# Weight conversion without its shared buffer, transposes of k and q in one buffer, and another order of a pair's steps, in a fused attention and channel-mixing kernel on one core

## The chip, the cores and the metric

The kernel runs on one core of a Trainium2 chip. Its time is the device time of the core in microseconds, and the time of a kernel is the median over its runs. Before the change three runs took 1230.66, 1232.53 and 1235.76 us. The lowest lies 0.15% below the median.

## The reference

Eight batches of eight heads, 576 tokens, head width 64. Each head goes through an attention with exponential features, the heads are laid side by side to 512 channels, and two mixing steps follow, one over tokens (rank 32) and one over channels (512 to 2048 to 512).

```python
def phi(x):
    proj = np.einsum('bhsd,df->bhsf', x, w_phi)              # 128 features
    proj = proj - np.max(np.abs(proj), axis=-1, keepdims=True)
    return np.concatenate([np.exp(proj), np.exp(-proj)], axis=-1)
q_p, k_p = (phi(q), phi(k))
kv = np.einsum('bhsf,bhsd->bhfd', k_p, v)
z = np.sum(k_p, axis=2)
num = np.einsum('bhsf,bhfd->bhsd', q_p, kv)
den = np.einsum('bhsf,bhf->bhs', q_p, z)[..., None] + 1e-06
x = num / den                                   # then heads to channels
h = x.transpose(0, 2, 1) @ U @ V                # over tokens
u = x + h.transpose(0, 2, 1)
out = u + np.maximum(u @ w_ch1, 0.0) @ w_ch2    # over channels
```

q, k, v and w_phi come as 32-bit floats. U, V, w_ch1 and w_ch2 come as 64-bit floats, which the chip converts itself from their words.

## The kernel before

**Pairs.** A `Pair` is two heads of one batch; there are 32, four to a batch. Its steps are: load of raw k and q (L250, L257); `transpose_k` (a small transpose tT of the 64 last tokens, and T0, k with features on partitions) and `transpose_q` (T1, the same of q); `s_k0` and `s_k1` (projection matmuls pkt and pk, then maxima, differences and exponentials of k); `s_kv` (kv_ps, the sums over tokens); `s_q0` and `s_q1` (pq, and the features of q, with the maximum over partitions on POOL, L342, and its subtraction on DVE, L343); and `s_out` (matmuls xp, then the division into x). From batch 2 on (`split`) a float is carried as two rounded parts: T is copied to a rounded upper half by ACT (L275), and the rest is written by DVE (L276). T0 and T1 have a buffer each (tags T0 and T1, L311).

**Tokens.** For a batch whose four pairs are done, `split` writes x as two parts (xs, three buffers of the group "wide" at a time), `down` multiplies with U (pp, kept as pst, L551 and L552), `up` multiplies with V (vp) and adds to x (L565), which also goes to memory.

**Mixer.** u is transposed (pt, split into uT_hi and uT_lo), then 16 pieces of 128 hidden channels follow. `hidden(f)` is a chunk of 12 matmuls into ph, from which ACT makes h_hi (L599) and DVE h_lo (L600). `add(f)` is a chunk of 12 matmuls into the four banks o. A batch thus has 32 chunks, kept in a list `todo`, from which `mix(n)` takes the next n. There are nine mixers: one a batch, and one for the last 64 tokens of all batches (x_tail).

**Weights.** `weight_blocks` converts 32 blocks of 128 by 512 words (m = 1, 2 and f = 0 to 15). A block is loaded from SP into a buffer of "wide" (512 KB, L216 or L220). ACT (L141, L145) and DVE (L142, L147, L150) take the words apart, POOL adds the two pieces (L155, INT64_ADD), ACT rounds the upper part w_hi (L226) and DVE writes the rest w_lo (L227). The piece that L147, L150 and L155 work on is w_r, one buffer for all blocks, so L147 of a block comes after L227 of the block before. "wide" has three buffers, which also hold xs and, at the end of each batch, the saved u (st).

**What sets the order.** Batches 0 and 1, with the weights, are ordered on every engine by a scheduler that simulates the program. From pair 8 on (`ordered`), the order on TensorE is the one written out: between two steps of the pairs stand one or two chunks of the batch before, and at a batch's end (`boundary`) the last three chunks alternate with the transposes of the next mixer. The other engines are still ordered by the scheduler. An engine runs its instructions strictly in its order. "cur", "nxt" and "far" are the pair that gives its output, the next, and the one after.

PSUM has eight banks: three of the group "at" (everything of the pairs and of Tokens, in turn), one ph, four o.

Of the kernel before, what the change touches and what calls it, by code (L numbers as in the profile page):

```python
# [20 lines left out]
P = 128  # L21
# [4 lines left out]
def tile_kernel(  # L26
# [96 lines left out]
    NW = 3  # L123
# [85 lines left out]
    def weight_blocks():  # L209

        for f in range(NFC):
            fs = slice(f * P, (f + 1) * P)
            for m in (1, 2):
                st = wide(f"w{m}_{f}", (C, 2), I32)
                if m == 1:
                    nc.sync.dma_start(  # L216
                        out=st.rearrange("p (c n) w -> p c n w", c=NCC),
                        in_=w1[:, fs].rearrange("(c p) n w -> p c n w", c=NCC))
# [7 lines left out]
                nc.scalar.copy(out=hi, in_=r)  # L226
                nc.vector.tensor_sub(lo, r, f32(hi))  # L227
                w_hi_t[m, f], w_lo_t[m, f] = hi, lo
            yield f
# [9 lines left out]
    class Pair:  # L239
# [38 lines left out]
        def transposes(self):  # L278
            self.transpose_k()
            self.transpose_q()  # L280

        def transpose_k(self):

            nm = self.nm
            tT = self.ps("tT", True)
            nc.tensor.transpose(out=tT[:, 0:2 * ST], in_=self.t_r, identity=ident)
            dt = F32R if self.split else F32
            self.tail_T = att.tile([P, 2, P], dt, tag="tail_T", name=f"tail_T{nm}")
            if not self.split:
                nc.gpsimd.memset(self.tail_T, 0.0)  # L290
            self.T = [self.transpose(0)]
# [11 lines left out]
        def transpose(self, n):  # L303
# [6 lines left out]
            if self.split:  # L310
                m = att.tile([P, 2, SM], F32R, tag=f"T{n}", name=f"T{n}_{self.nm}")  # L311
                for s in range(2):
                    self.stack(pT[s * D:(s + 1) * D, :], m[:, s, :])
            else:
                m = att.tile([P, SM], F32, tag=f"T{n}", name=f"T{n}_{self.nm}")
                nc.scalar.copy(out=m, in_=pT)
# [252 lines left out]
    class Mixer:  # L569
# [35 lines left out]
        def add(self, f):  # L605
            if self.o is None:
                self.o = [ps(f"o{self.g}_{t}", "o") for t in range(4)]
            terms = self.h.pop(f)
            for t in range(4):
# [11 lines left out]
            if f == NFC - 1:  # L621
                self.finish()

        def finish(self):
            g = self.g
            for t in range(4):
# [7 lines left out]
                if t % 2 == 1:  # L634

                    tails = out[2 * t - 2:2 * t + 2, SM:S, :].rearrange(
                        "(t s) r e -> s r t e", s=2)
                    for s in range(2):
                        nc.sync.dma_start(
                            out=tails[s], in_=self.x[s * ST:(s + 1) * ST, t - 1:t + 1, :])  # L640
# [20 lines left out]
    def mix(n=1):  # L661
        for _ in range(n):
            if todo:
                fn, f = todo.pop(0)
                if fn.__self__.g == 0 and done_f[0] < NFC:
                    weights(f + 2)
                fn(f)
# [81 lines left out]
    def boundary(m, up=None, far=None):  # L749

        mix(len(todo) - 3)
        m.transposes(0)
        m.transposes(1)
        mix()
        m.transposes(2)
        mix()
        if up is not None:
            up(NT)
        m.transposes(3)
        mix()  # L760
        todo.extend(m.chunks())
        mix()
        if far is not None:
            far.transpose_q()

    def ordered(cur, nxt, x, xt, tk):

        for n, (b, j) in list(enumerate(pairs))[ORDERED * NPAIR:]:
# [10 lines left out]
            mix()  # L779
            do(nxt, "s_k1")  # L780
            mix()
# [8 lines left out]
            if j == 1:  # L790
                tk.down(0)
            if last:
                mix()
                tk.down(1)
            do(nxt, "s_q1")
            do(far, "transpose_k")
            mix()
            if last:
# [13 lines left out]
            else:  # L812
                do(far, "transpose_q")
                mix(2 if j == 2 else 1)
# [6 lines left out]
    if True:  # L821
# [4 lines left out]
        cur.transposes()  # L826
# [4 lines left out]
        nxt.transposes()  # L831
# [6 lines left out]
        for n, (b, j) in enumerate(pairs[:ORDERED * NPAIR]):  # L838
# [5 lines left out]
            if nxt.split:  # L844
                step(nxt.s_k1)
            step(narrow, nxt, cur, x, xt)
            if j == 1:
                tk.split(0)
            if j == NPAIR - 1:
                fill = [nxt.s_q0] + ([nxt.s_q1] if nxt.split else []) + [far.transposes]  # L850
# [7 lines left out]
            else:  # L858
# [3 lines left out]
                step(far.transposes)  # L862
            cur, nxt = nxt, far
        with tc.manual_schedule(engines={nc.tensor.engine}):
            mix(3)
# [32 lines left out]
```

## Time and profile before

| what | us |
|---|---|
| runs: lowest, median, highest | 1230.66, 1232.53, 1235.76 |
| the profiled execution, as a run | 1234.6 |
| its span in the trace | 1232.8 |
| TensorE busy (PE) | 1159.0 |
| VectorE busy (DVE) | 652.4 |
| ScalarE busy (ACT) | 534.7 |
| GpSimd busy (POOL) | 197.0 |
| mean granted clock of TensorE | 0.982 |

The span is what the trace covers; 1.8 us of the run lie around it. TensorE is busy almost throughout, yet not evenly: the page's row of 40 slices is well under full in the first quarter and full after it. In the first 280 us lie batches 0 and 1, the loading and conversion of the weights and all 32 chunks of the first mixer; the rest is batches 2 to 7 in the hand-written order (to about 1005 us) and, behind them, the last mixers alone. A row of a timeline gives the start in us, the duration in us, the engine, the line, the operation and tiles, and in brackets how long the engine stood idle before it and what ended that.

### The profile page before, as it was taken

Reading aid. Unit: us, or ns where it says so; the run is one execution under the profiler, and the core shown is the slowest. Engines: PE = TensorE matmul, PEld = TensorE weight load, DVE = VectorE, ACT = ScalarE, POOL = GpSimd, SP = SyncE. Lnnn points to the kernel's source line nnn. Section 1 sums busy time; section 2 is a strip of 40 time slices with the busy share of each in tenths; the row PEclk is TensorE's granted clock in tenths of the full one; section 3 lists DMA queues with packets and bytes.
Section 4 is the critical chain, followed back from the end, with each engine's and each line's share of the span. In section 5 each row is a group of like instructions: output and inputs, shape, how many; then the busy total and the mean of one; then the engine's idle time right before and its main releaser. Section 6 shows DMA issues by size and latency. Waiting matters only on the chain.

```text
span 1232.8 us, 22555 instructions
## 1 busy us (share of the span) xinstructions
PE 1159.0 (94%) x9316; PEld 951.2 (77%) x9316; DVE 652.4 (53%) x1339; ACT 534.7 (43%) x1134; POOL 197.0 (16%) x151
## 2 busy tenths in 40 slices
PE   7988797879999999999999999999999999999998
PEld 5767575647888888888887888888888788888886
DVE  6666586955653665556655655466636633212111
ACT  5776565734543355435553545355434532101110
POOL 2423332321111111102210112011111110000000
PEclk8988898989999999999999999999999999999999
DMA  4343343431112111211112111311122002200001
GB/s 115 83 147 102 102 131 104 128 132 30 30 31 90 60 46 31 89 57 31 41 45 100 32 38 30 118 38 31 32 88 71 7 2 86 90 1 8 27 1 35
DMA packets 90470, 75.75 MB, mean 61 GB/s; under 512 B 51584, under 2 KB 76672, under 8 KB 90240
## 3 DMA queue, kind: packets, MB, share of 16 engines
q1 hardware_dynamic: 90368, 74.31, 20.1%
q8 instruction: 74, 1.21, 0.4%
q14 instruction: 28, 0.23, 0.1%
HBM read 55.41 MB, written 18.87 MB: 60 GB/s over the span
## 4 chain that ended last, share of the span: by engine, by line
PE 74%; DVE 11%; ACT 6%; DMA 6%; POOL 1%; issue 1%; SPq 1%; POOLq 0%; DVEq 0%; ACTq 0%
PE ph L593 27%; PE o L612 27%; DMA w<-in_moe_w_ch_dram 5%; PE xp L459 5%; PE kv_ps L434 4%; DVE T L276 2%; DVE qp L343 2%; PE pk L391 2%; PE pp L548 1%; PE T L307 1%; PE pt L580 1%; DVE w_r L150 1%; ACT T L275 1%; PE kv_ps L424 1%; POOL w_r L155 1%
## 5 line engine op out<-in xcount | busy, mean ns | idle before, releaser
L612 PE MATMUL o<-w_hi,h_hi 128*128 128x512 f32 x576 | 229.1, 405 | 18.0 <-ACT h_hi L599 12.9
L600 DVE SCALAR_TENSOR_TENSOR h_lo<-ph,h_hi 128x512 fp32r<-128x512 f32 x144 | 99.3, 690 | 267.3 <-ACT h_hi L599 267.1
L593 PE MATMUL ph<-uT_hi,w_hi 128*128 128x512 f32 x576 | 232.5, 404 | 7.1 <-ACT w_hi L226 5.6
L593 PE MATMUL ph<-uT_hi,w_lo 128*128 128x512 f32 x576 | 226.9, 394 | 0.0
L599 ACT ACTIVATE h_hi<-ph 128x512 fp32r<-128x512 f32 x144 | 85.9, 596 | 324.8 <-PE ph L593 324.3
L593 PE MATMUL ph<-uT_lo,w_hi 128*128 128x512 f32 x576 | 226.0, 392 | 0.3 <-DVE uT_lo L234 0.3
L612 PE MATMUL o<-w_lo,h_hi 128*128 128x512 f32 x576 | 225.9, 396 | 0.3 <-DVE w_lo L227 0.3
L612 PE MATMUL o<-w_hi,h_lo 128*128 128x512 f32 x576 | 225.0, 398 | 0.5 <-DVE h_lo L600 0.5
L612 PEld LDWEIGHTS o<-w_hi,h_hi 128*128 128x128 f32 x576 | 109.0, 191 | 44.3 <-ACT h_hi L599 16.2
L342 POOL PARTITION_ALL_REDUCE qp<-qp x64 | 128.0, 2010 | 73.1 <-ACT qp L341 71.5
L593 PEld LDWEIGHTS ph<-uT_hi,w_hi 128*128 128x128 f32 x576 | 109.0, 189 | 32.3 <-ACT w_hi L226 8.9
L612 PEld LDWEIGHTS o<-w_hi,h_lo 128*128 128x128 f32 x576 | 110.1, 192 | 25.7 <-DVE h_lo L600 2.1
L593 PEld LDWEIGHTS ph<-uT_hi,w_lo 128*128 128x128 f32 x576 | 108.7, 189 | 26.2 <-DVE w_lo L227 2.5
L612 PEld LDWEIGHTS o<-w_lo,h_hi 128*128 128x128 f32 x576 | 110.0, 191 | 22.0 <-DVE w_lo L227 0.7
L593 PEld LDWEIGHTS ph<-uT_lo,w_hi 128*128 128x128 f32 x576 | 109.1, 189 | 20.8 <-DVE uT_lo L234 0.7
L342 POOL PARTITION_ALL_REDUCE qp_t<-qp_t x32 | 25.6, 799 | 600.1 <-ACT qp_t L341 600.1
L276 DVE TENSOR_TENSOR T<-T,T 64x512 fp32r<-64x512 f32 x96 | 66.1, 689 | 18.2 <-ACT T L275 16.6
L459 PE MATMUL xp<-kv,qp 128*64 128x65 f32 x2048 | 71.0, 228 | 1.4 <-ACT qp L344 0.7
L459 PEld LDWEIGHTS xp<-kv,qp 128*64 128x64 f32 x2048 | 66.8, 143 | 4.9 <-issue 2.5
L434 PEld LDWEIGHTS kv_ps<-vb,kp 128*64 128x64 f32 x2048 | 65.9, 138 | 5.8 <-issue 2.9
L434 PE MATMUL kv_ps<-vb,kp 128*64 128x65 f32 x2048 | 68.8, 223 | 0.1
L332 ACT ACTIVATE kp<-kp 128x512 f32<-128x512 f32 x64 | 40.4, 633 | 60.7 <-DVE kp L329 60.6
(127 smaller groups left out, 1504.3 us busy)
## 6 DMA issues: line engine op xcount, KB each, us to landing
w<-in_moe_w_ch_dram SPq DMA_DIRECT2D x32, 512.0 KB, 3.7
raw<-in_k_dram SPq DMA_DIRECT2D x32, 256.0 KB, 3.0
raw<-in_q_dram SPq DMA_DIRECT2D x32, 256.0 KB, 2.7
vb<-in_v_dram SPq DMA_DIRECT2D x64, 128.0 KB, 2.9
u_dram<-x SPq DMA_DIRECT2D x32, 256.0 KB, 2.6
st<-u_dram SPq DMA_DIRECT2D x16, 512.0 KB, 4.1
out_dram<-st SPq DMA_DIRECT2D x32, 256.0 KB, 2.4
t_r<-in_k_dram SPq DMA_DIRECT2D x32, 32.0 KB, 2.1
```

The costliest lines, as they stand in the source:

```text
L150: nc.vector.scalar_tensor_tensor(out=a, in0=hi_w, scalar=-0x80000000, in1=a, op0=ALU.bitwise_and, op1=ALU.bitwise_or)
L276: nc.vector.tensor_sub(dst[D:2 * D], src, f32(dst[0:D]))
L332: nc.scalar.activation(out=kp[:, :, 0:F], in_=kp[:, :, F:2 * F], func=AF.Exp)
L342: nc.gpsimd.partition_all_reduce(qp[:, 0, :], qp[:, 1, :], P, ReduceOp.absmax)
L343: nc.vector.tensor_sub(qp[:, 1, :], qp[:, 1, :], qp[:, 0, :])
L391: nc.tensor.matmul(pk[:, i, :, :], self.T[0][:, i, cs], w_hl, start=True, stop=True)
L434: nc.tensor.matmul(self.kv_v[z * HP:(z + 1) * HP, f, g, :], kp[:, i, f * F + z * HP:f * F + (z + 1) * HP], self.vb[:, g, t, :], start=Fals ...
L459: nc.tensor.matmul(xv[zs, c, :], qp[:, f, c * P + z * HP:c * P + (z + 1) * HP], self.kv[:, f, c // 2, :], start=(f == 0), stop=(f == 1), s ...
L593: nc.tensor.matmul(ph, l[:, c * P:(c + 1) * P], r[:, c, :], start=(n == 0), stop=(n == len(terms) * NCC - 1))
L599: nc.scalar.activation(out=h_hi, in_=ph, func=AF.Relu)
L600: nc.vector.scalar_tensor_tensor(out=h_lo, in0=ph, scalar=0.0, in1=f32(h_hi), op0=ALU.max, op1=ALU.subtract)
L612: nc.tensor.matmul(self.o[t], l[:, cs], r, start=(f == 0 and n == 0), stop=(f == NFC - 1 and n == len(terms) - 1))
```

## The change

1. w_r gets no buffer of its own: it lies in the buffer that becomes w_lo of the next block (tags wl0 to wl32). L147 of a block then waits no more for L227 of the block before. "wide" gets a fourth buffer.
2. T0 and T1 of a pair use one buffer (tag T), one after the other; before batch 2, where they are not split, one tile holds both.
3. In `ordered`, `transpose_q` of nxt comes after `s_k1`, one chunk later, and `transpose_k` of far right after `s_q1`, with two chunks behind it. `boundary` places the first transpose of a mixer ahead of its chunk, the other parts elsewhere, `transpose_k` of far late, and takes the next mixer's first hidden chunk in before the last add is complete.
4. The last two adds of every mixer but the first run in two halves of six matmuls, each with its own output; the mixer of the last tokens writes eight transfers of 128 KB in place of four of 256 KB.

```diff
-    NW = 3
+    NW = 4
...
             for m in (1, 2):
+                i = 2 * f + m - 1
...
-                r = const.tile([P, C], F32, tag="w_r", name=f"w_r{m}_{f}")
+                r = const.tile([P, C], F32, tag=f"wl{i + 1}", name=f"w_r{m}_{f}")
                 convert(st, r.bitcast(I32), b_, True)
                 hi = const.tile([P, C], F32R, tag=f"wh{m}_{f}", name=f"w_hi{m}_{f}")
-                lo = const.tile([P, C], F32R, name=f"w_lo{m}_{f}")
+                lo = const.tile([P, C], F32R, tag=f"wl{i}", name=f"w_lo{m}_{f}")
...
-                m = att.tile([P, 2, SM], F32R, tag=f"T{n}", name=f"T{n}_{self.nm}")
+                m = att.tile([P, 2, SM], F32R, tag="T", name=f"T{n}_{self.nm}")
...
-        def add(self, f):
+        def add(self, f, ts=range(4)):
...
             if f == NFC - 1:
-                self.finish()
+                self.finish(ts)
...
+                for s in range(2):
+                    nc.sync.dma_start(
+                        out=out[2 * t + s, SM:S, :], in_=self.x[s * ST:(s + 1) * ST, t, :])
...
-                todo.append((self.add, f))
+                if self.g > 0 and f >= NFC - 2:
+                    todo += [(self.add, f, ts) for ts in ((0, 1), (2, 3))]
+                else:
+                    todo.append((self.add, f))
...
-    def boundary(m, up=None, far=None):
-
-        mix(len(todo) - 3)
+    def boundary(m, early=None, late=None):
+
+        mix(len(todo) - 5)
+        if early is not None:
+            early(2)
+            early(3)
         m.transposes(0)
+        mix()
         m.transposes(1)
-        mix()
         m.transposes(2)
         mix()
-        if up is not None:
-            up(NT)
         m.transposes(3)
         mix()
-        todo.extend(m.chunks())
+        if early is not None:
+            early(NT)
+        if late is not None:
+            late()
         mix()
-        if far is not None:
-            far.transpose_q()
+        new = m.chunks()
+        todo.insert(0, new.pop(0))
+        todo.extend(new)
+        mix()
...
             do(nxt, "s_k0")
-            mix()
+            mix(2 if j == 0 else 1)
             do(nxt, "s_k1")
+            if not last:
+                mix()
+            do(nxt, "transpose_q")
             mix()
             narrow(nxt, cur, x, xt)
...
             do(nxt, "s_q0")
             mix()
-            if j == 1:
-                tk.down(0)
-            if last:
+            do(nxt, "s_q1")
+            if not last:
+                do(far, "transpose_k")
+                mix()
+                if j == 1:
+                    tk.down(0)
+                mix()
+            else:
                 mix()
                 tk.down(1)
-            do(nxt, "s_q1")
-            do(far, "transpose_k")
-            mix()
-            if last:
+                mix()
                 tk.up(0)
                 tk.up(1)
                 mix()
-                tk.up(2)
-                tk.up(3)
-                mix()
-                boundary(Mixer(b, x), tk.up, far)
+                boundary(Mixer(b, x), tk.up, far.transpose_k if far is not None else None)
...
-            else:
-                do(far, "transpose_q")
-                mix(2 if j == 2 else 1)
```

The rows that follow are instructions in the order of one engine: line, operation, tile written and tiles read (the numbers behind a name are batch, pair or piece, and a running number), and the shape. A line of "..." leaves rows out.

**TensorE at a pair of batch 3**, before. T0 and T1 of pair 3_2 stand one chunk apart, and the chunk of o is all that lies between T1 and the pair's first projections:

```order
L416 MATMUL pq1_3_1_4578<-T1_3_1_4350,w_hl_2381 128x512
L286 MATMUL tT3_2_4587<-ident_79,t_r3_2_4360 128x128
L307 MATMUL T0_3_2_4590<-ident_79,raw3_2_0_4356 128x128 x4
L593 MATMUL ph2_3_4604<-uT_hi2_4229,w_hi1_3_1443 128x512
...
L307 MATMUL T1_3_2_4621<-ident_79,raw3_2_1_4358 128x128 x4
L612 MATMUL o2_0_4425<-w_hi2_2_1412,h_hi2_2_4544 128x512
...
L353 MATMUL pkt3_2_4654<-w_hl_2381,tail_T3_2_4589 128x128
L391 MATMUL pk00_3_2_4664<-w_hl_2381,T0_3_2_4595 128x256 x2
L391 MATMUL pk01_3_2_4669<-w_hl_2381,T0_3_2_4595 128x256 x2
```

and after, the same pair:

```order
L416 MATMUL pq1_3_1_4587<-T1_3_1_4428,w_hl_2363 128x512
L283 MATMUL tT3_2_4596<-ident_79,t_r3_2_4332 128x128
L308 MATMUL T0_3_2_4599<-ident_79,raw3_2_0_4328 128x128 x4
L612 MATMUL o2_0_4407<-w_hi2_2_1406,h_hi2_2_4446 128x512
...
L593 MATMUL ph2_4_4625<-uT_hi2_4212,w_hi1_4_1522 128x512
...
L353 MATMUL pkt3_2_4653<-w_hl_2363,tail_T3_2_4598 128x128
L391 MATMUL pk00_3_2_4663<-w_hl_2363,T0_3_2_4604 128x256 x2
...
L391 MATMUL pk11_3_2_4696<-w_hl_2363,T0_3_2_4604 128x256 x2
...
L308 MATMUL T1_3_2_4723<-ident_79,raw3_2_1_4330 128x128 x4
...
L424 MATMUL kv_ps3_2_4795<-vt0_85,kp3_2_t_4656 64x130 x4
```

T1 has moved behind pk11 and a chunk; between T0 and pk00 now stand two whole chunks and no other transposes, and between T1 and kv_ps one chunk (of o) and the matmuls xp.

**DVE ahead of the first mixer**, before. pst0 is the second half of `down` of batch 0, on which its `up` and the first mixer wait:

```order
L535 TENSOR_TENSOR xs0_1_2_1073<-x0_337,xs0_1_2_1073 128x256
L441 COPY kv1_0_1062<-kv_ps1_0_1025 128x260
L343 TENSOR_TENSOR qp1_0_t_1083<-qp1_0_t_1083 128x128
L552 TENSOR_TENSOR pst0_704<-pp0_1_1131,pst0_704 32x256
L343 TENSOR_TENSOR qp1_0_0_1093<-qp1_0_0_1093 128x512
L565 TENSOR_TENSOR x0_337<-x0_337,vp0_0_1147 128x512
```

and after:

```order
L142 TENSOR_SCALAR w_b1_0_1328<-w1_0_1326 128x512
...
L150 SCALAR_TENSOR_TENSOR w_r1_0_1329<-w1_0_1326,w_r1_0_1329 128x512
...
L142 TENSOR_SCALAR w_b2_0_1342<-w2_0_1340 128x512
...
L150 SCALAR_TENSOR_TENSOR w_r2_0_1343<-w2_0_1340,w_r2_0_1343 128x512
L228 TENSOR_TENSOR w_lo2_0_1351<-w_r2_0_1343,w_hi2_0_1350 128x512
L441 COPY kv1_0_1057<-kv_ps1_0_1020 128x260
L142 TENSOR_SCALAR w_b1_1_1356<-w1_1_1354 128x512
...
L142 TENSOR_SCALAR w_b2_1_1370<-w2_1_1368 128x512
L147 TENSOR_SCALAR w_r2_1_1371<-w2_1_1368 128x512
L150 SCALAR_TENSOR_TENSOR w_r2_1_1371<-w2_1_1368,w_r2_1_1371 128x512
L343 TENSOR_TENSOR qp1_0_0_1088<-qp1_0_0_1088 128x512
L552 TENSOR_TENSOR pst0_701<-pp0_1_1125,pst0_701 32x256
```

Four blocks now stand ahead of pst0. On SP the loads of blocks w2_0, w1_1 and w2_1 each wait for DVE and ACT to be done with the block before, since all four take the same buffer of "wide", while the other three hold xs of batch 0.

**DVE in the middle of the weights**, before, without a break, at blocks w1_4 to w2_5:

```order
L147 TENSOR_SCALAR w_r1_4_1521<-w1_4_1518 128x512
L150 SCALAR_TENSOR_TENSOR w_r1_4_1521<-w1_4_1518,w_r1_4_1521 128x512
L227 TENSOR_TENSOR w_lo1_4_1529<-w_r1_4_1521,w_hi1_4_1528 128x512
L147 TENSOR_SCALAR w_r2_4_1535<-w2_4_1532 128x512
L142 TENSOR_SCALAR w_b2_5_1652<-w2_5_1650 128x512
L150 SCALAR_TENSOR_TENSOR w_r2_4_1535<-w2_4_1532,w_r2_4_1535 128x512
L227 TENSOR_TENSOR w_lo2_4_1543<-w_r2_4_1535,w_hi2_4_1542 128x512
L147 TENSOR_SCALAR w_r1_5_1639<-w1_5_1636 128x512
```

and after:

```order
L150 SCALAR_TENSOR_TENSOR w_r1_4_1515<-w1_4_1512,w_r1_4_1515 128x512
L142 TENSOR_SCALAR w_b1_5_1631<-w1_5_1629 128x512
L147 TENSOR_SCALAR w_r1_5_1632<-w1_5_1629 128x512
...
L228 TENSOR_TENSOR w_lo1_3_1438<-w_r1_3_1430,w_hi1_3_1437 128x512
...
L150 SCALAR_TENSOR_TENSOR w_r2_4_1529<-w2_4_1526,w_r2_4_1529 128x512
L142 TENSOR_SCALAR w_b2_5_1645<-w2_5_1643 128x512
L147 TENSOR_SCALAR w_r2_5_1646<-w2_5_1643 128x512
L150 SCALAR_TENSOR_TENSOR w_r1_5_1632<-w1_5_1629,w_r1_5_1632 128x512
L228 TENSOR_TENSOR w_lo2_3_1452<-w_r2_3_1444,w_hi2_3_1451 128x512
```

A block's rest (L228) now stands behind the first steps of two to three later blocks, and of a later block only that block's own L228 needs it done.

More of the change, by code (lines that the diff above doesn't have):

```diff
@@ L276, in stack @@
             nc.vector.tensor_sub(dst[D:2 * D], src, f32(dst[0:D]))
-        def transposes(self):
-            self.transpose_k()
-            self.transpose_q()
         def transpose_k(self):
@@ L290, in transpose_k @@
                 nc.gpsimd.memset(self.tail_T, 0.0)
-            self.T = [self.transpose(0)]
+            if self.split:
+                self.T = [self.transpose(0)]
+            else:
+                both = att.tile([P, 2, SM], F32, tag="T", name=f"T_{nm}")
+                self.T = [self.transpose(n, both[:, n, :]) for n in range(2)]
             for g in range(2):
@@ L301, in transpose_q, with transpose @@
             self.T.append(self.transpose(1))
-        def transpose(self, n):
+        def transpose(self, n, m=None):
             pT = self.ps(f"T{n}_", True)
@@ L314, in transpose @@
             else:
-                m = att.tile([P, SM], F32, tag=f"T{n}", name=f"T{n}_{self.nm}")
                 nc.scalar.copy(out=m, in_=pT)
@@ L603, in hidden @@
             self.h[f] = ((h_hi, w_hi), (h_hi, w_lo), (h_lo, w_hi))
-        def add(self, f):
+        def add(self, f, ts=range(4)):
             if self.o is None:
                 self.o = [ps(f"o{self.g}_{t}", "o") for t in range(4)]
-            terms = self.h.pop(f)
-            for t in range(4):
+            terms = self.h[f]
+            for t in ts:
                 cs = slice(t * P, (t + 1) * P)
@@ L621, in add, with finish @@
             if f == NFC - 1:
-                self.finish()
-        def finish(self):
+                self.finish(ts)
+        def finish(self, ts):
             g = self.g
-            for t in range(4):
+            for t in ts:
                 if g < B:
@@ L633, in finish @@
                 nc.vector.tensor_add(self.x[:, t, :], self.x[:, t, :], self.o[t])
[L634 to L640, printed above, removed]
+                for s in range(2):
+                    nc.sync.dma_start(
+                        out=out[2 * t + s, SM:S, :], in_=self.x[s * ST:(s + 1) * ST, t, :])
         def chunks(self):
@@ L663, in mix @@
             if todo:
-                fn, f = todo.pop(0)
+                fn, f, *ts = todo.pop(0)
                 if fn.__self__.g == 0 and done_f[0] < NFC:
                     weights(f + 2)
-                fn(f)
+                fn(f, *ts)
     class Pace:
@@ L789, in ordered @@
             mix()
-            if j == 1:
-                tk.down(0)
-            if last:
+            do(nxt, "s_q1")
[5 more added lines that the diff above has]
+                mix()
+            else:
                 mix()
                 tk.down(1)
-            do(nxt, "s_q1")
-            do(far, "transpose_k")
-            mix()
-            if last:
+                mix()
                 tk.up(0)
@@ L825, in tile_kernel @@
         keep_busy(6)
-        cur.transposes()
+        cur.transpose_k()
         cur.s_k0()
@@ L830, in tile_kernel @@
         nxt.load_v()
-        nxt.transposes()
+        nxt.transpose_k()
         load_uv()
@@ L845, in tile_kernel @@
                 step(nxt.s_k1)
+                nxt.transpose_q()
             step(narrow, nxt, cur, x, xt)
@@ L849, in tile_kernel @@
             if j == NPAIR - 1:
-                fill = [nxt.s_q0] + ([nxt.s_q1] if nxt.split else []) + [far.transposes]
+                fill = [nxt.s_q0] + ([nxt.s_q1] if nxt.split else []) + [far.transpose_k]
                 tokens(tk, fill)
@@ L861, in tile_kernel @@
                     step(tk.down, 0)
-                step(far.transposes)
+                step(far.transpose_k)
             cur, nxt = nxt, far
         with tc.manual_schedule(engines={nc.tensor.engine}):
-            mix(3)
+            mix(2)
             ordered(cur, nxt, x, xt, tk)
```

## The prediction

> **What bounds the kernel now.** I read the page first, then busy time by stretches, then the waits of TensorE, then single stretches of the chain and of the timeline. On the page TensorE is busy 94% of the span, but the 40 slices show that the missing part lies early:
>
> ```profile
> PE 1159.0 (94%) x9316; PEld 951.2 (77%) x9316; DVE 652.4 (53%) x1339; ACT 534.7 (43%) x1134; POOL 197.0 (16%) x151
> PE   7988797879999999999999999999999999999998
> ```
>
> The stretches (start and end, length, busy time of PE, PEld, DVE, ACT and POOL, then granted clock, DMA share, GB/s) separate the stages:
>
> ```profile
> 92.60:280.40 187.80, 155.83 (x1055) 113.99 (x1051) 127.75 (x242) 107.94 (x199) 60.96 (x44) 0.93 0.36 114
> 280.40:1005.00 724.60, 702.89 (x6208) 594.30 (x6209) 416.53 (x858) 332.01 (x739) 105.46 (x69) 1.00 0.17 50
> 411.70:542.00 130.30, 126.55 (x1102) 106.96 (x1102) 75.22 (x155) 59.60 (x134) 18.51 (x12) 1.00 0.18 54
> ```
>
> The first stretch is the first mixer, from its first h_lo to the first h_lo of the second. The last is one steady batch: 32 chunks and four pairs, nearly the same work, in 126.55 us of TensorE and 3.75 idle. So the first mixer takes 187.8 - 126.55 = 61 us more than TensorE needs at full clock. The ordered part (second row) idles 724.6 - 702.9 = 21.7 us in all. Behind 1005 us there are only chunks, and nothing to win but the last transfer. The change touches both stages, and the stretch before 92.6 us.
>
> What holds the first mixer is the weights. The chain there, in order of time (start, us):
>
> ```profile
> 139.98 3.54 DMA w<-in_moe_w_ch_dram
> 143.55 0.47 DVE w_b L142
> 144.02 0.58 DVE w_r L150
> ...
> 144.66 3.63 DMA w<-in_moe_w_ch_dram
> 148.31 0.47 DVE w_b L142
> ...
> 149.41 3.43 DMA w<-in_moe_w_ch_dram
> ```
>
> A load starts when L150 of the block before is done, and L150 of the next comes after that load: 144.66 - 139.98 = 4.7 us a block. A second circle has the same length, through the single w_r (durations min/median/max in ns):
>
> ```profile
> L147 DVE TENSOR_SCALAR w_r<-w x32: 404/426/1276, 80.0 to 264.4; 128x512 int32<-128x512 int32 x32
> L150 DVE SCALAR_TENSOR_TENSOR w_r<-w,w_r x32: 673/684/1637, 83.2 to 264.9; 128x512 int32<-128x512 int32 x32
> L155 POOL INT64_ADD w_r<-w_r,w_b x32: 1264/1288/1577, 84.1 to 265.8; - x32
> L226 ACT CAST w_hi<-w_r x32: 592/617/622, 86.3 to 267.1; 128x512 fp32r<-128x512 f32 x32
> L227 DVE TENSOR_TENSOR w_lo<-w_r,w_hi x32: 669/692/1227, 87.0 to 267.8; 128x512 fp32r<-128x512 f32 x32
> ```
>
> 0.43 + 0.68 + 1.29 + 0.62 + 0.69 = 3.7 us, and hand-overs and other rows of DVE between. DVE itself works only 0.47 + 0.43 + 0.68 + 0.69 = 2.3 us a block.
>
> **The ordered part.** TensorE's waits there (total us, times, longest):
>
> ```profile
> PE pk L391 <- DVE T L276: 11.1, 12, 1.0
> PE pk L391 <- DVE kp_t L329: 4.9, 5, 1.0
> PE T L307 <- ACT qp L341: 2.8, 5, 0.6
> PE T L307 <- DVE pst L552: 2.1, 6, 0.3
> ```
>
> Together 20.9 us, all of the idle time but the hand-overs. A pair shows the mechanism:
>
> ```profile
> 432.22 0.60 PE L307 MATMUL T<-ident,raw 128*128 128x128 f32 x4
> 432.58 0.48 PE L612 MATMUL o<-w_hi,h_hi 128*128 128x512 f32 x1
> ...
> 436.95 0.47 PE L391 MATMUL pk<-w_hl,T 128*128 128x256 f32 x2 [0.92 <-DVE T L276]
> ...
> 435.13 0.69 DVE L343 TENSOR_TENSOR qp<-qp 128x512 f32<-128x512 f32 x1
> ...
> 436.11 0.69 DVE L276 TENSOR_TENSOR T<-T,T 64x512 fp32r<-64x512 f32 x1
> ...
> 443.30 0.45 PE L452 MATMUL xp<-kv,qp_t 128*64 128x65 f32 x8
> ...
> 445.45 0.61 PE L424 MATMUL kv_ps<-vt,kp_t 128*64 128x130 f32 x8
> 1204.95 2.72 PE o L612 x12
> ```
>
> T1 leaves TensorE at 432.58 and its PSUM bank is emptied at 436.11 + 0.69 = 436.80, 4.2 us later, since DVE has L343 of the pair before in between. One chunk is 2.72 us, so pk, which needs that bank, waits. After the change pk00 has two chunks in front of it since T0, 5.4 us against 4.2 at worst. T1's bank is wanted next by kv_ps, one chunk and the xp matmuls later: 2.72 + (445.45 - 443.30) = 4.9 us against 4.2. Both fit, the second by 0.7 us. With T1 gone from there, the first, third and fourth row have no cause left, and the second (pk01 behind the small kp_t) has its DVE rows earlier. At the six boundaries the pieces stand one chunk from what needs them. I take 17 of the 20.9. The bounds are 21 (all go, nothing new) and 8 (only three quarters of the 11.1 row go, the rest comes back at kv_ps). The shared buffer T adds two waits, of the copy L275 for the last pk and for the last pq that read it. On TensorE the last pk stands a chunk ahead of T1's transposes and the last pq right ahead of T0's, so both are over by the time that a copy could start: nothing. Were they not, h_hi would stand behind the copy on ACT, and the chunk of o behind h_hi.
>
> The halved last adds reorder the same matmuls: nothing, hidden by the ones around them. The end has four additions and a transfer after the last matmul:
>
> ```profile
> 1224.71 2.72 DVE x_tail L633 x4
> ```
>
> There transfers of half the size can start each one addition (0.7 us) earlier, but there are twice as many to issue: 0 to 1.4 us, I take 0.5.
>
> **The stretch before the first mixer.** Here the order gets worse. Now (rows of SP and DVE):
>
> ```profile
> 59.19 1.50 SPq L267 DMA_DIRECT2D vb<-in_v_dram  x2
> ...
> 66.93 0.42 DVE L535 TENSOR_TENSOR xs<-xt,xs 128x256 fp32r<-128x256 f32 x1
> ...
> 74.82 0.42 DVE L552 TENSOR_TENSOR pst<-pp,pst 32x256 fp32r<-32x256 f32 x1 [3.46 <-ACT pst L551]
> ...
> 92.59 0.69 DVE L600 SCALAR_TENSOR_TENSOR h_lo<-ph,h_hi 128x512 fp32r<-128x512 f32 x1 [1.45 <-ACT h_hi L599]
> ```
>
> and all loads of weights come after 74 us:
>
> ```profile
> L216 SPq DMA_DIRECT2D w<-in_moe_w_ch_dram x16: 367/373/560, 74.2 to 246.5; - x16
> ...
> DMA to landing us min/median/max: 3.4/3.7/7.0
> ```
>
> In the new order DVE has the first four blocks ahead of pst0. w1_0 can be loaded behind vb, at about 60.7, so its steps follow the xs row and end near 68.7. Three more go through the same buffer one by one: 3.7 landing + 0.47 + 0.43 + 0.58 = 5.2 us each, to 84.3. pst0 then comes near 85, **+10 us**. Behind the waiting L142 stand kv1_0, the differences of q and pst0; behind pst0 the whole of `up`, and behind the waiting loads on SP those of raw and v for batch 1. If the engines pass each other better, DVE is late by only one round (5 us); with slower landings (7.0 is the longest) by 15.
>
> Between pst0 and the first h_lo DVE has 50 rows with 28.3 us of durations, where it had 32 with 17.6. **+8**, since a little of it fills idle time (bounds 0 and 11).
>
> Third, these blocks run side by side with POOL, which they did not before. What that costs, DVE's rows beside POOL's show:
>
> ```profile
> 98.83 4.21 POOL L342 PARTITION_ALL_REDUCE qp<-qp  x2 [1.24 <-ACT qp L341]
> ...
> 99.00 1.28 DVE L147 TENSOR_SCALAR w_r<-w 128x512 int32<-128x512 int32 x1
> ...
> 101.17 1.64 DVE L150 SCALAR_TENSOR_TENSOR w_r<-w,w_r 128x512 int32<-128x512 int32 x1
> ...
> 159.07 1.31 POOL L155 INT64_ADD w_r<-w_r,w_b  x1 [3.71 <-DVE w_r L150]
> ...
> 159.37 1.30 DVE L535 TENSOR_TENSOR xs<-xt,xs 128x256 fp32r<-128x256 f32 x1
> ```
>
> L147 took 1.28 instead of 0.43, L150 1.64 instead of 0.68, L535 1.30 instead of 0.42: 0.9 us each. In the old order POOL's addition stands between DVE's steps of the same block, so they rarely meet; in the new one L150 or L228 of another block stands there. One meeting a block is my estimate, eight blocks here: **+7** (bounds 0 and 1.3 x 8 = 10). Sum of the stretch: 10 + 8 + 7 = **+25**, bounds +5 and +35.
>
> **The first mixer.** With four buffers, w_r apart, and some 14 blocks done by its second chunk, no circle of 4.7 us is left. It needs TensorE's 126.5 and the 3.75 that a steady batch idles; meetings for the other 18 blocks, of which about 0.55 us a block lies on the path, 10; the second group of blocks starts with loads one by one, 3 left over after cover; and restarts at a lower clock, 4.5 (the clock was 0.93 in this stretch). Sum 148 instead of 187.8: **-40**. Bounds: 130 (-57), all covered, and 161 (-27), where each meeting costs POOL's full 1.3 us and no chunk hides it.
>
> The Trainium skill, SBUF — State Buffer, "Who interferes with whom", has a rule for such meetings: a DVE instruction with two SBUF inputs and a GpSimd instruction that reads SBUF exclude each other, and the later is blocked until the other has ended. By that rule the row at 159.37 is right (it ends 0.29 us after POOL's), while the row at 99.00 ended amid two reductions. Taken whole, the rule would put 1.3 us on each block, the third rival below.
>
> **Sum** against the profiled execution: 1234.6 + 25 - 40 - 17 - 0.5 = 1202.1. That execution is 2.1 above the median of the runs, so the forecast is **1200 us**.
>
> **The rivals.**
> - *No meetings.* If POOL's additions fall beside idle time of DVE, the 7 and the 10 go: 1183. For it: only one row in many is long now, L150's median is 0.684 with a longest of 1.64. Against: those rows come from an order that keeps them apart.
> - *Loads still set the pace.* The scheduler's order on DVE lets one late load hold everything behind it; then the mixer gains only its lower bound, -27 against +25, and the bank waits move to kv_ps instead of going. 1232.5 - 2 = 1230, the change not doing what it says.
> - *Full exclusion.* Each addition of 1.3 us stops DVE in full: start +3, mixer +13 more, 1216.
> - *Slower: the T hand-over.* The shared buffer and T1 near kv_ps make both hand-overs late by the 0.92 us of the row above, twice a pair, 24 pairs: 44 against 20.9 saved, +23; with the first stretch as in the second rival, 1253. It decides where T1's bank is emptied over 4.9 us after its matmuls; it is 4.2 now, and L343, which makes it late, moves away from it. So this is unlikely.
>
> **How the numbers follow.** A difference of 0.5% (6 us) is about what a measurement of this kernel can tell from no change: below 1226.4 is faster, above 1238.7 slower. Chances: forecast 0.48, no meetings 0.21, full exclusion 0.14, loads 0.10, hand-over 0.07. The range reaches from 1177 (6 under the no-meetings case) to 1226, and leaves out the slower rival, most of the loads case and a margin below. Faster: the first three but for 0.02 at the edge, 0.81; same 0.10; slower 0.09.
>
> **What would show it.** Right: pst0 near 85 and the first h_lo near 117, the second mixer's first h_lo 148 after it; L150, L228 and L343 with means well over their medians; no row of pk waiting for T among TensorE's waits, and a steady batch of about 127.5 instead of 130.3. Wrong: first h_lo before 100 (start term), a mixer still at 170 or more with w_lo or w_b waits of DVE near the 4.7 us cycle, or new waits of kv_ps or T in the ordered part.

## The result and the profile after

The changed kernel takes 1195.26 us (median of four runs, 1194.9 to 1196.7), the kernel before 1232.35 in the same comparison: a ratio of 0.970, with a 95% interval of 0.968 to 0.972. The profiled execution took 1194.9 us, with a span of 1193.1. Its page shows the first third better filled, with the weak slices pulled together near the start:

```profile
PE 1140.7 (96%) x9308; PEld 947.4 (79%) x9316; DVE 661.1 (55%) x1339; ACT 529.2 (44%) x1134; POOL 200.5 (17%) x151
PE   7966998989999999999999999999999999999997
```

The stretches of the changed kernel, cut at the first h_lo of the first mixer and of the second (columns as in the prediction), and one row of the kernel before that starts at its second cut:

```profile
60.00:116.30 56.30, 36.67 (x384) 26.33 (x382) 47.02 (x86) 41.34 (x75) 21.83 (x15) 0.82 0.52 169
116.30:266.10 149.80, 134.68 (x957) 105.37 (x957) 117.71 (x212) 89.93 (x174) 49.30 (x35) 0.95 0.34 108
266.10:1193.10 927.00, 919.38 (x7270) 777.97 (x7270) 456.88 (x934) 358.94 (x792) 107.62 (x69) 1.00 0.16 47
...
280.40:1232.80 952.40, 924.60 (x7266) 777.97 (x7266) 463.81 (x937) 363.95 (x796) 106.37 (x69) 1.00 0.15 46
```

The first mixer lasts 149.8 instead of 187.8 us, the rest of the program 927.0 instead of 952.4. Against that the first mixer starts 23.8 us later. Its start in the changed kernel, on DVE's timeline:

```profile
70.83 0.46 DVE L142 TENSOR_SCALAR w_b<-w 128x512 uint16<-128x512 uint16 x1 [0.72 <-DMA w<-in_moe_w_ch_dram]
...
76.27 0.46 DVE L142 TENSOR_SCALAR w_b<-w 128x512 uint16<-128x512 uint16 x1 [0.81 <-DMA w<-in_moe_w_ch_dram]
...
86.10 0.42 DVE L552 TENSOR_TENSOR pst<-pp,pst 32x256 fp32r<-32x256 f32 x1 [1.62 <-ACT pst L551]
...
116.34 0.68 DVE L600 SCALAR_TENSOR_TENSOR h_lo<-ph,h_hi 128x512 fp32r<-128x512 f32 x1
```

The blocks ahead of pst0 follow each other at the distance of one load and its steps, 76.27 - 70.83 = 5.4 us, and pst0 comes at 86.1 instead of 74.8. Of TensorE's waits from 270 us on one is left (total us, times, longest); another wait for h_lo, 1.4 us, lies just ahead, at the start of the second mixer:

```profile
PE ph L593 <- DVE h_lo L600: 0.3, 1, 0.3
```

### The profile page after: what moved, and what is told of

Its sections match the earlier page's. It is cut to its first block, busy times and chain, and to the rows that moved or that the text cites. A ratio compares the mean times of both kernels' runs of the same rounds, so it can differ in the third digit from the quotient of the medians.

```text
span 1193.1 us, 22535 instructions
## 1 busy us (share of the span) xinstructions
PE 1140.7 (96%) x9308; PEld 947.4 (79%) x9316; DVE 661.1 (55%) x1339; ACT 529.2 (44%) x1134; POOL 200.5 (17%) x151
## 4 chain that ended last, share of the span: by engine, by line
PE 83%; DVE 9%; DMA 3%; ACT 2%; issue 1%; SPq 1%; POOL 0%; POOLq 0%; DVEq 0%; ACTq 0%
PE ph L593 31%; PE o L612 31%; PE xp L459 4%; PE kv_ps L434 4%; DMA w<-in_moe_w_ch_dram 2%; PE T L308 2%; PE pk L391 2%; DVE w_r L150 1%; PE pp L548 1%; DVE w_lo L228 1%; DVE w_b L142 1%; PE pt L580 1%; PE kv_ps L424 1%; DVE w_r L147 1%; PE pq L415 1%
## 5 line engine op out<-in xcount | busy, mean ns | idle before, releaser
L612 PE MATMUL o<-w_hi,h_hi 128*128 128x512 f32 x576 | 233.0, 405 | 4.1 <-ACT h_hi L599 4.1
L612 PE MATMUL o<-w_hi,h_lo 128*128 128x512 f32 x576 | 220.5, 392 | 0.0
L612 PEld LDWEIGHTS o<-w_hi,h_lo 128*128 128x128 f32 x576 | 107.6, 188 | 23.4 <-DVE h_lo L600 0.3
L276 ACT CAST T<-T 64x512 fp32r<-64x512 f32 x96 | 55.9, 582 | 36.8 <-PE T L308 20.4
L434 PE MATMUL kv_ps<-vb,kp 128*64 128x65 f32 x2048 | 66.1, 222 | 0.0
```

The lines of the kernel that those rows point to most:

```text
L276: nc.scalar.copy(out=dst[0:D], in_=src)
L434: nc.tensor.matmul(self.kv_v[z * HP:(z + 1) * HP, f, g, :], kp[:, i, f * F + z * HP:f * F + (z + 1) * HP], self.vb[:, g, t, :], start=Fals ...
L612: nc.tensor.matmul(self.o[t], l[:, cs], r, start=(f == 0 and n == 0), stop=(f == NFC - 1 and n == len(terms) - 1))
```

## The experiments

Twelve kernels ran, each timed beside the kernel before (1233.4 to 1234.1 us in these comparisons). The table has the stages of the profiled executions: the start of pst0, the first h_lo of the first and of the second mixer, and what follows it to the end of the span. Ratios are to the kernel before, with 95% intervals.

| kernel | us | ratio | pst0 | first h_lo | second mixer | rest |
|---|---|---|---|---|---|---|
| before | 1232.4 | 1 | 74.8 | 92.6 | 280.4 | 952.4 |
| after | 1195.3 | 0.970 (0.968 to 0.972) | 86.1 | 116.3 | 266.1 | 927.0 |
| order_only | 1210.1 | 0.982 (0.980 to 0.984) | 73.9 | 91.2 | 280.7 | 926.4 |
| weights_only | 1222.3 | 0.992 (0.990 to 0.994) | 75.0 | 101.5 | 267.7 | 952.7 |
| three_wide | 1190.1 | 0.966 (0.964 to 0.968) | 78.4 | 105.3 | 261.7 | 926.8 |
| one_w_r | 1201.1 | 0.976 (0.973 to 0.978) | 87.2 | 106.9 | 271.6 | 926.7 |
| late_loads | 1189.9 | 0.965 (0.963 to 0.967) | | | | |
| half_add | 1183.5 | 0.960 (0.958 to 0.962) | 88.3 | 113.8 | 254.3 | 926.5 |
| t1_late | 1223.1 | 0.992 (0.990 to 0.994) | 86.6 | 116.9 | 266.8 | 954.0 |
| two_T | 1194.1 | 0.967 (0.965 to 0.970) | 74.8 | 101.6 | 265.2 | 926.7 |
| t1_early | 1193.2 | 0.967 (0.966 to 0.969) | 73.5 | 100.6 | 265.5 | 927.7 |
| dve_add | 1185.1 | 0.960 (0.958 to 0.962) | 79.6 | 102.5 | 257.8 | 926.5 |
| flip | 1229.1 | 0.996 (0.995 to 0.997) | 73.9 | 91.3 | 278.6 | 948.6 |
| dve_add_late | 1177.6 | 0.955 (0.953 to 0.956) | 77.2 | 101.4 | 247.2 | 926.5 |

In late_loads the profiled execution ran TensorE at less than half its speed (843 ns for a matmul of ph, 404 in the kernel before), so its trace is not used, and its time is the median of the three other runs.

### The parts apart

**order_only** puts the weights and T back:

```diff
-    NW = 4
+    NW = 3
-                r = const.tile([P, C], F32, tag=f"wl{i + 1}", name=f"w_r{m}_{f}")
+                r = const.tile([P, C], F32, tag="w_r", name=f"w_r{m}_{f}")
-                m = att.tile([P, 2, SM], F32R, tag="T", name=f"T{n}_{self.nm}")
+                m = att.tile([P, 2, SM], F32R, tag=f"T{n}", name=f"T{n}_{self.nm}")
```

> The changed kernel with w_r, the three buffers of wide and the two buffers of T put back; only the order of the steps, the halves and the last transfers are new. My account of the two traces gives the ordered part 25.4 us, independent of the weights: 1232.4 - 25.4 = 1207 us, with the first h_lo of the second mixer at 280 as before. Rival (the shared T buffer or the way in which the first mixer ends carries a part of it): 1212 us or more.

**weights_only** is the kernel before with w_r moved and nothing else:

```diff
-                r = const.tile([P, C], F32, tag="w_r", name=f"w_r{m}_{f}")
+                r = const.tile([P, C], F32, tag=f"wl{i + 1}", name=f"w_r{m}_{f}")
-                lo = const.tile([P, C], F32R, name=f"w_lo{m}_{f}")
+                lo = const.tile([P, C], F32R, tag=f"wl{i}", name=f"w_lo{m}_{f}")
```

> The kernel before with only w_r moved into the next block's place (three buffers of wide, old order). Theory: w_r was the circle and the fourth buffer is not needed; nothing stands ahead of pst0 (near 75), the first h_lo comes near 103 and the second mixer's first h_lo near 258: 1232.4 - 22 = 1210 us. Rival (a load is issued only after L150 of the block before, so the 4.7 us a block stay): 1230 us, first h_lo of the second mixer near 280.

order_only came out at 1210.1, with the second mixer at 280.7 as before and the rest at 926.4. weights_only has the rest of the kernel before, 952.7, and the second mixer 13 us earlier. So the two parts act in different stretches: the order is worth 25 to 26 us behind the second mixer's first h_lo whatever the weights do (23 by the medians of order_only), and the weights shift that point. They do not simply add: moving w_r gains 11 us in the old order (weights_only) and 16 in the new one (from order_only to two_T, below). Of weights_only the pst0 and the first h_lo came as expected (75 and 101), but the mixer took 166 us instead of 155, so it gained 11 us, not 22.

**three_wide** takes the fourth buffer away from the changed kernel, **one_w_r** puts the one w_r back into it:

```diff
-    NW = 4
+    NW = 3
```

> The changed kernel with three buffers of wide instead of four. Theory: the fourth buffer lets four blocks in ahead of pst0, one by one, and costs the start more than it brings: pst0 back near 75, first h_lo near 103, 1195.3 - 10 = 1185 us. Rival (four buffers are what takes the loads off the circle): 1205 us or more, with waits of DVE for loads.

```diff
-                r = const.tile([P, C], F32, tag=f"wl{i + 1}", name=f"w_r{m}_{f}")
+                r = const.tile([P, C], F32, tag="w_r", name=f"w_r{m}_{f}")
```

> The changed kernel with the one w_r put back, four buffers of wide kept. Theory: start still late (pst0 near 86), and the circle through w_r of 4.7 us a block is back, so the first mixer lasts near 180: 1195.3 + 20 to 25 = 1215 to 1220 us. Rival (the fourth buffer carries the gain): 1197 us.

three_wide is 5 us faster than the changed kernel: the fourth buffer, as it is used there, costs time. The size is half of what I expected. one_w_r refutes both expectations: it loses 6 us, neither 20 to 25 nor 2, and yet the circle is back. The rows of w_r in order_only, one_w_r, three_wide and the changed kernel (first and last start stand behind the durations) show how:

```profile
L147 DVE TENSOR_SCALAR w_r<-w x32: 402/426/1275, 79.0 to 265.1; 128x512 int32<-128x512 int32 x32
...
L147 DVE TENSOR_SCALAR w_r<-w x32: 406/426/1424, 67.3 to 256.0; 128x512 int32<-128x512 int32 x32
...
L147 DVE TENSOR_SCALAR w_r<-w x32: 401/411/1765, 82.6 to 239.1; 128x512 int32<-128x512 int32 x32
...
L147 DVE TENSOR_SCALAR w_r<-w x32: 402/410/1522, 66.1 to 235.3; 128x512 int32<-128x512 int32 x32
```

With one w_r the 32 blocks take 186.1 and 188.7 us, with three buffers or four: the pace is w_r's. But with four they start 11.7 us earlier, ahead of pst0, and end 9.1 earlier. I had counted the late pst0 as a loss alone; where the blocks' chain sets the end, an early start of it is a gain. With w_r moved, the blocks take 156.5 us (three_wide) and 169.2 (after): there the early start brings only 3.8 us at the end of the blocks, while the first h_lo comes 11.0 us later, and the second mixer 4.4 later.

Counted to the second mixer's first h_lo, from order_only's 280.7, w_r moved without the fourth buffer is worth 19.0 us (three_wide; 15.5 in two_T, which has order_only's two buffers of T), the fourth buffer without w_r moved 9.1 (one_w_r), and both together 14.6 (after). Either one takes most of the excess off the first mixer's length, from 189.5 us to 156.4 or 164.7, so that gain cannot be given to one of them alone. And with w_r moved the blocks no longer come evenly: in the changed kernel L147 twice starts 27 to 28 us after the one before it (120.2 to 147.3 and 195.7 to 223.8 us), where the longest such distance was 14.9 us before. What sets the first mixer's length now is open.

**late_loads** keeps four buffers and holds the fourth until pst0:

```diff
             self.xs = []
+            if b == 0 and i == 1:
+                self.hold = wide("hold", (16,))
+                nc.vector.memset(self.hold, 0.0)
...
+            if b == 0 and i == 1:
+                nc.vector.tensor_tensor(
+                    out=warm[lo, 1:2], in0=self.hold[lo, 0:1],
+                    in1=f32(self.pst[lo, C // 2:C // 2 + 1]), op=ALU.add)
```

> The changed kernel, in which the fourth buffer of wide is held by a small dummy tile until pst0 is done, so no block can start ahead of pst0 (one tiny addition on DVE more). Theory: the four blocks ahead of pst0 are what made the start late, and the four buffers are good for the rest: pst0 near 75, first h_lo near 105 as with three buffers, first mixer near 150 as in the changed kernel, second mixer's first h_lo near 256: 1185 us. Rival (blocks that aren't done early are paid in the first mixer): second h_lo near 262 to 266, 1190 to 1195 us.

At 1189.9 it equals three_wide (1190.1), so the theory's 1185 was missed and the rival came closer: the early blocks are what made the fourth buffer cost 5 us, and beyond that the buffer brought nothing as long as POOL adds. That rests on the times alone; the stages of late_loads are not known.

**two_T** is three_wide with a buffer for T0 and one for T1:

```diff
-                m = att.tile([P, 2, SM], F32R, tag="T", name=f"T{n}_{self.nm}")
+                m = att.tile([P, 2, SM], F32R, tag=f"T{n}", name=f"T{n}_{self.nm}")
```

> The kernel with three buffers of wide (1190.1 us), and T0 and T1 in buffers of their own again. Theory: sharing the buffer adds no wait, it only pays for space: the ordered part stays at 926.8 us, the whole within 2 us but for the scheduler's other order of the weights (weights_only had that order and its second h_lo at 267.7 instead of 261.7: then 1196 us). Rival (sharing costs waits of the copies L276): 1185 us, by a shorter ordered part.

The ordered part is 926.7 against 926.8: sharing adds no wait. The 4 us lost lie ahead of the second mixer (265.2 against 261.7), where the scheduler puts the weights into nearly the order that weights_only has. What sharing brings is space: a T takes 4 KB of a partition, as much as the fourth buffer of wide.

### The meetings on DVE

In the changed kernel, POOL's additions and DVE's rows at about 103 and 107 us:

```profile
103.18 1.28 POOL L155 INT64_ADD w_r<-w_r,w_b  x1 [1.06 <-ACT w_hi L227]
107.06 1.30 POOL L155 INT64_ADD w_r<-w_r,w_b  x1 [2.60 <-ACT w_b L145]
...
103.53 1.48 DVE L228 TENSOR_TENSOR w_lo<-w_r,w_hi 128x512 fp32r<-128x512 f32 x1
...
107.15 1.49 DVE L147 TENSOR_SCALAR w_r<-w 128x512 int32<-128x512 int32 x1
```

Both of DVE's rows started while an addition ran and ended 0.55 and 0.28 us after it. Seventeen rows of these steps began while a single addition ran and took over 0.25 us longer than usual, and all of them ended so: 0.28 to 0.34 us after the addition where the row has one input in SBUF (L142, L147), 0.55 where it has two (L150, L228). The groups (total us and mean ns stand behind the first bar), first of the kernel before, then of the changed kernel, then L147 of dve_add_late, where POOL adds nothing:

```profile
L227 DVE TENSOR_TENSOR w_lo<-w_r,w_hi 128x512 fp32r<-128x512 f32 x32 | 22.6, 707 | 30.3 <-ACT w_hi L226 30.0
L150 DVE SCALAR_TENSOR_TENSOR w_r<-w,w_r 128x512 int32<-128x512 int32 x32 | 22.9, 715 | 0.3
L142 DVE TENSOR_SCALAR w_b<-w 128x512 uint16<-128x512 uint16 x32 | 16.6, 518 | 12.1 <-DMA w<-in_moe_w_ch_dram 11.7
L147 DVE TENSOR_SCALAR w_r<-w 128x512 int32<-128x512 int32 x32 | 14.7, 460 | 0.5
...
L228 DVE TENSOR_TENSOR w_lo<-w_r,w_hi 128x512 fp32r<-128x512 f32 x32 | 27.6, 862 | 8.6 <-ACT w_hi L227 8.2
L150 DVE SCALAR_TENSOR_TENSOR w_r<-w,w_r 128x512 int32<-128x512 int32 x32 | 25.0, 780 | 0.3
L142 DVE TENSOR_SCALAR w_b<-w 128x512 uint16<-128x512 uint16 x32 | 22.4, 699 | 4.4 <-DMA w<-in_moe_w_ch_dram 4.3
L147 DVE TENSOR_SCALAR w_r<-w 128x512 int32<-128x512 int32 x32 | 19.5, 610 | 0.0
...
L147 DVE TENSOR_SCALAR w_r<-w 128x512 int32<-128x512 int32 x32 | 13.3, 416 | 0.0
...
L600 DVE SCALAR_TENSOR_TENSOR h_lo<-ph,h_hi x144: 678/691/694, 116.3 to 1181.7; 128x512 fp32r<-128x512 f32 x144
```

The four groups take 94.5 us; before the change the same four took 76.8. The last row, h_lo of the changed kernel, reads one input from PSUM, and not one of its 144 instructions is long, though six of the early ones run beside POOL, three of them beside an addition. The Trainium skill, SBUF — State Buffer, "Who interferes with whom", says just that: a DVE instruction with two SBUF inputs, or one in a mode that uses both port pairs, excludes a GpSimd instruction that reads SBUF, and one with at most one SBUF input outside such modes does not. L147 has one SBUF input and was held, so by that rule it ran in such a mode; no run here shows the mode itself.

**half_add** lets POOL add half of each block and leaves the addition out for the other half; in **dve_add** (three buffers) and **dve_add_late** (late_loads) DVE adds:

```diff
-            nc.gpsimd.int64_add(a64, a64, b64)
+            h64 = slice(0, a64.shape[1] // 2)
+            nc.gpsimd.int64_add(a64[:, h64], a64[:, h64], b64[:, h64])
```

> The changed kernel with POOL adding only the first half of each block's words (the weights are then wrong in the other half), in nearly the same order on DVE. INT64_ADD should fall from 1.3 to about 0.7 us. Theory (meetings with POOL lengthen DVE's all-SBUF rows, 23.6 us over their shortest in the changed kernel): the excess falls to about half, and the second mixer's first h_lo comes 6 to 10 us earlier: 1186 to 1189 us. Rival (the excess is waiting that other things cover): within 2 us of 1195.

```diff
-                convert(st, r.bitcast(I32), b_, True)
+                convert(st, r.bitcast(I32), b_)
```

> The kernel with three buffers of wide (1190.1 us), and DVE doing the blocks' addition itself, in 32 bits, in place of POOL. That adds 32 rows of about 0.69 us to DVE and takes away 32 additions of 1.3 us on POOL and the rows that they lengthen (30 us over their shortest). Theory (meetings cost as much as the addition would on DVE): second h_lo within 6 us of 261.7, 1185 to 1192 us, most likely 1186. Rival (DVE's own work sets the pace, meetings do not): +15 us, 1205 us.

> late_loads (four buffers, held until pst0 is done) with DVE doing the blocks' addition. Theory (DVE's work and not the loads set the first mixer's pace, so a fourth buffer brings nothing, as in late_loads): within 3 us of dve_add's 1185.1. Rival (with no meetings the loads show, and the fourth buffer pays): 1178 us.

half_add's four groups fall by 13.4 us to 81.1, and the kernel by 11.8, more than the 6 to 10 expected. dve_add gains 5.0 us on three_wide, although DVE has 32 rows more (here those of dve_add_late):

```profile
L157 DVE CUSTOM_DVE_ANT_0 w_r<-w_r,w_b 128x1024 uint16<-128x1024 uint16 x32 | 21.6, 678 | 0.3
```

And dve_add_late went the way of the rival: with the meetings gone the fourth buffer pays 7.6 us, and the kernel is the fastest here, 1177.6 us, 17.7 under the changed one. How much of these gains is the meetings and how much the shorter way through a block (in dve_add and dve_add_late 0.68 us on DVE in place of 1.3 on POOL and a hand-over) isn't separated: all three kernels shorten both.

### The ordered part

**t1_late** moves T1 a chunk back:

```diff
             if not last:
                 mix()
-            do(nxt, "transpose_q")
             mix()
+            do(nxt, "transpose_q")
             narrow(nxt, cur, x, xt)
```

> The changed kernel with transpose_q one chunk later in the hand-written order, right ahead of the xp matmuls. Theory (what waits is the PSUM bank: T1's bank is empty 3.4 us after its transposes, the xp matmuls give only 2.15): kv_ps now waits about 1.3 us in each pair of batches 2 to 7, and each gap costs some 0.16 us of overlap more: 23 pairs, +30 to +35, 1225 to 1230 us, the price that the slower rival of the prediction had. Rival (another bank is free in time): 1195 us.

It loses 27.9 us, of which 27.0 in the ordered part. A pair, on the timelines of TensorE and DVE, and the stretch behind the second mixer's first h_lo:

```profile
435.11 0.60 PE L308 MATMUL T<-ident,raw 128*128 128x128 f32 x4
...
438.49 0.66 PE L424 MATMUL kv_ps<-vt,kp_t 128*64 128x130 f32 x8 [0.53 <-PE xp L459]
...
437.69 0.69 DVE L277 TENSOR_TENSOR T<-T,T 64x512 fp32r<-64x512 f32 x1 [0.23 <-ACT T L276]
...
266.80:1220.80 954.00, 923.31 (x7270) 782.64 (x7270) 456.74 (x934) 359.27 (x792) 107.62 (x69) 1.00 0.16 46
```

kv_ps starts 0.11 us after T1's bank is empty (437.69 + 0.69). The row in brackets names xp, which merely came last in the profile's account; DVE's row shows the true releaser. The 23 waits of kv_ps add 23.1 us of idle time, 1.0 each where 1.3 was expected, and 923.31 - 919.38 = 3.9 us of busy time, 0.17 for each gap.

**t1_early** puts T1 back to its old place in three of four pairs (two_T being the base):

```diff
-            do(nxt, "transpose_q")
+            if nxt is not None and len(nxt.T) == 1:
+                nxt.transpose_q()
...
                 do(far, "transpose_k")
                 mix()
+                do(far, "transpose_q")
```

> The two_T kernel with T1 one chunk behind T0 again in three of four pairs (as before the change), one chunk ahead of pk; boundary, halves and the rest as in the changed kernel. Theory (T1's place is what made pk wait): pk's wait for T is back, 0.92 us in the 12 pairs that showed it, and each gap costs 0.16 us of TensorE's overlap more: ordered part 926.7 + 11.1 + 2 = 940 us, the whole 1207 us. Rival (the gain of the ordered part lies in the boundary and the other places): ordered part under 931 us, the whole 1195 us.

The theory fell: no wait of pk came back, the ordered part is 927.7. At the pair that corresponds to the one of the prediction, T1 stands at 415.86, a chunk ahead of pk as before, and its bank is empty at 419.24, 3.4 us after its transposes started, where it was 436.80 - 432.22 = 4.6 before the change:

```profile
415.86 0.60 PE L308 MATMUL T<-ident,raw 128*128 128x128 f32 x4
419.22 0.69 PE L391 MATMUL pk<-w_hl,T 128*128 128x256 f32 x4
...
418.55 0.69 DVE L277 TENSOR_TENSOR T<-T,T 64x512 fp32r<-64x512 f32 x1
```

What differs is the chunk between T0 and T1: o here, a hidden chunk before. (One pair a batch of t1_early has a hidden chunk there and yet no wait; in it the ten matmuls pp stand between T1 and pk besides a chunk, and pk comes 4.5 us after T1's transposes started instead of 3.4.) ACT's timeline, before the change and then in t1_early:

```profile
432.80 0.60 ACT L599 ACTIVATE h_hi<-ph 128x512 fp32r<-128x512 f32 x1
433.29 0.62 ACT L345 ACTIVATE qp<-qp 128x512 f32<-128x512 f32 x1
433.81 0.57 ACT L275 CAST T<-T 64x512 fp32r<-64x512 f32 x1
...
416.49 0.58 ACT L276 CAST T<-T 64x512 fp32r<-64x512 f32 x1
```

Before, that chunk's h_hi and an exponential of q stood ahead of T1's first copy, which began 1.6 us after T1's transposes had; in t1_early it begins 0.6 after them. **flip** tests the kind of chunk in the kernel before, with T1 left alone:

```diff
         todo.extend(m.chunks())
-        mix()
+        mix(2)
         if far is not None:
             far.transpose_q()
```

> The kernel before with one edit: at the end of a boundary two hidden chunks of the next mixer run instead of one, so that in the first two pairs of a batch a chunk of o stands between T0 and T1 and a hidden chunk behind T1, where it was the other way round; T1 keeps its place. Theory after t1_early (the h_lo of the hidden chunk between T0 and T1 is what held T1's bank on DVE): pk's wait for T (11.1 us, 12 times) goes, and 0.16 us a gap with it: 1233.5 - 13 = 1220 us, ordered part near 939. Rival (T1's place): 1233 us, the wait stays.

TensorE's waits in its ordered part:

```profile
PE ph L593 <- DVE h_lo L600: 7.8, 6, 1.4
PE pk L391 <- DVE kp_t L329: 4.9, 5, 1.0
...
PE pk L391 <- DVE T L276: 1.9, 2, 0.9
```

The wait for T fell from 11.1 us to 1.9, as expected, but the two hidden chunks in a row brought a new one of 7.8 for h_lo, and the kernel gained 4 us. So with T1 in its old place the kind of chunk ahead of it decides that wait, and the gain stays only where no other wait takes its place. Whether moving T1 alone, with a hidden chunk left between, would have ended the wait too, no run shows. The other rows (kp_t, qp, pst) I didn't take apart, nor the halves of the last adds.

## Why the prediction was right

1200 us were forecast in a range of 1177 to 1226, and 1195.3 came. The two large terms of the sum came within 2 us each and the third was 8 us too small; the causes behind them were only in part the ones named. Step by step, from the profiled executions:

- **Start, +25.** It was +23.8 (92.59 to 116.34): pst0 11.3 later instead of 10, and from there 12.5 longer instead of 8 + 7. The serial loads, the added rows of DVE (50 in this stretch, as forecast) and the meetings were all there. But the early blocks are only a part of it. The late pst0 goes with the fourth buffer (86.1 and 87.2 with it, 78.4 in three_wide without). The longer way from pst0 to the first h_lo goes with w_r: 26.9 us in three_wide and 26.5 in weights_only, which have no early blocks, and 19.7 in one_w_r, which has them, against 17.8 before and 30.2 after.
- **First mixer, -40.** It was -38.1 (187.8 to 149.7). The parts of the 21.5 us that I put above TensorE's 126.5 no run separates. Of the 38.1, TensorE's idle time gave 16.9 (32.0 to 15.1) and its busy time 21.2 (155.83 to 134.68). Part of the latter is no gain: 98 matmuls fewer lie in the stretch and 80 more ahead of it, where TensorE is busy 86.6 us instead of 78.6. The late start and the short mixer share these 8 us, so that both terms fit as well as they do is in part luck; their sum, -14.3 against -15, is the firmer figure. The gain was given to w_r and four buffers alike; to the second mixer's first h_lo w_r moved alone is worth more than both (three_wide), and the fourth buffer, in the place it has, takes back 4 to 5.
- **Ordered part, -17.** This term was mis-sized: 25.4 with the end. My upper bound, the 21 us of waits, is no bound, because I took TensorE's busy time as fixed: a steady batch was to take 127.5 us, and the one of the prediction's row took 125.5 (391.23 to 516.73), less than the 126.55 for which TensorE alone was busy in it before. Idle time behind the second h_lo fell by 20.2 us (27.8 to 7.6, the differences of the two rows above), and TensorE's busy time by 5.2 (924.60 to 919.38) with the same matmuls. A gap costs more than it shows. Before, the pk of one pair stood in two pieces around a gap; after, they are one:

```profile
435.59 0.45 PE L391 MATMUL pk<-w_hl,T 128*128 128x256 f32 x2
...
390.49 0.69 PE L391 MATMUL pk<-w_hl,T 128*128 128x256 f32 x4
```

  0.45 and 0.47 (the row at 436.95 in the prediction) make 0.92, against 0.69: 0.23 us in the overlap of neighbours that the gap took. t1_late measured it from the other side, 0.17 a gap.
- **T1's place.** That T1's bank held pk is shown by the trace, and that it holds kv_ps once T1 comes a chunk later by t1_late. But the wait did not need T1's move in order to go: t1_early has T1 back in its place and no wait, and flip ends most of the wait by the alternation of chunks alone, which the edits had shifted too. The prediction didn't see that shift. How the other waits (kp_t, qp, pst: 9.8 us) went is open.
- **The shared T, 0.** Right (two_T).
- **The end, -0.5.** Wrong in sign: +0.5. From the first of the last four additions to the end of the span were 8.1 us (1224.71 to 1232.8), now 8.6 (1184.50 to 1193.1). Eight transfers take SP longer to issue than four, 5.02 us instead of 3.10:

```profile
1226.10 3.10 SPq L639 DMA_DIRECT2D out_dram<-x_tail  x4
...
1185.22 5.02 SPq L635 DMA_DIRECT2D out_dram<-x_tail  x8
```

- **The rivals.** Meetings came, so the first is out. The four groups grew by 17.7 us over 32 blocks, 0.55 a block, where the prediction took a lengthening of 0.9 in each; full exclusion would be 1.3. That the sum's 7 + 10 is nearly the same number confirms nothing, since it counts only what lies on the path, which no run separates. The means stood over the medians as forecast (L150 780 and 682 ns, L228 862 and 692, L343 859 and 693; L343's mean was 779 before). The slower rival's mechanism is real, as t1_late shows; its point of decision wasn't reached.

## What to carry to other kernels

Where a chain of equal steps sets the pace, ask both what closes its circle and when it starts: opening the circle brought the second mixer 13 to 19 us forward here, and an earlier start won 9 us or lost 4, depending on what is queued behind the early steps. Before a buffer is added, see in the order which early work it will let in, and after a change that runs two engines side by side, look at the mean duration of every group: rows that grew are a cost that no wait shows. And a wait that goes need not go for the reason of the edit; put the edit back alone and see whether it returns.

## What the hardware showed unexpectedly

A gap of TensorE cost 0.17 (t1_late, mean of 23) to 0.23 us (one pk before the change) beyond its idle time. DVE's single-input rows on integer words in SBUF (L142, L147) were lengthened by POOL's additions as much as those with two inputs: in the changed kernel from 0.46 and 0.41 to 1.5 us, where L150 went from 0.68 to 1.76. And DVE adds a block's words in 0.68 us, where POOL takes 1.3.
